# The first front of a two-layer attention and state-space kernel: time steps behind the first rows, square root's table first, a fifth bank, moduli ahead of sines

## The chip, the core and the metric

The kernel runs on one core of a Trainium2 chip. The metric is the time of one execution in device microseconds, as the median of several runs. Traces come from one profiled execution.

## The reference

The input is 2048 rows of 640 numbers. Four blocks follow each other, attention, state space, attention, state space, each on normalised rows and added to its input:

```python
x = x + _A_ref(_layernorm(x), A_wqkv, A_wo)      # 32 heads of 20, softmax(q k' / sqrt(20)) v, times wo
x = x + _B_ref(_layernorm(x), ...)
x = x + _A_ref(_layernorm(x), A_wqkv, A_wo)
x = x + _B_ref(_layernorm(x), ...)

# inside _B_ref: a convolution along the rows with one kernel K per channel d
dt = exp(log_dt)                                  # 640 time steps
A  = -exp(log_A_real) + 1j * A_imag               # 640 x 128
P  = exp((A * dt[:, None])[:, :, None] * pos)     # pos = 0 .. 2047
K  = 2.0 * einsum("dn,dnl->dl", C * dt, P).real
y  = irfft(rfft(u, 4096) * rfft(K, 4096))[:2048] + u * D_skip
```

## The kernel before

Each layer has four stages: a front, the attention proper, the output projection, and the state-space convolution. The kernels K are the same in both layers and depend on the weights alone, so they are made once, by the generator `kgen`, whose steps are woven into the first layer: its small tables are made in the first front, its products during the first attention.

**A front** normalises and transposes the rows. It runs over four groups `i4` of 512 rows (four row tiles `xr` of 128). For a group, VectorE takes the statistics (`ln_stats`: `bn_stats`, `bn_aggr`, then `rstd`: `va`, a square root on ScalarE into `lt`, a reciprocal and one correction into `rs`), and makes `nb`, minus the mean times `rs`. ScalarE applies `rs` and `nb` to each row tile. TensorE transposes the result in five columns `ct` of 128 channels, each into one PSUM tile `pst` of pool S (four buffers). ScalarE copies a column to `xh` (16 bits), and VectorE makes the rest `xl`. Then `block0` makes queries and keys of the first heads (`pq`, also in pool S, 15 products each), and `values4` the values (`pv`) of the group before, in pool M (two buffers, tag `mm`), copied out to `V` by VectorE and ScalarE in parts. Weights go through the same splitting: `stage` loads them and `make` produces `wh` on ScalarE or VectorE and `wl` on VectorE. After the last group the norms of queries and keys give a shift per row (`norms`, `longest`, `shift`), which is written to memory and loaded again as a part of the score operands. The last values end the front.

**The attention** makes a tile `S` of scores on TensorE, its exponential `pt` on ScalarE (128x1024, 2048 of them in both layers) and the weighted values on TensorE. It needs the banks that the front's pools held.

**`kgen`** first loads the tables `lar`, `aim` and `dsk` and the time steps `d5`, and makes the steps' exponential (`exp_exact`: a polynomial on VectorE beside one exponential on ScalarE). The steps go to memory and come back to all partitions (`dt`). Then come, for twelve powers `LV[n]`, `modulus(n)` (one exponential of 128x640 on ScalarE and a transfer to memory, `wd`) and `angle(n)` (four VectorE instructions, a sine and a cosine, both by ScalarE's sine, two transfers). The tiles of each kind have two buffers. `act[0]` ties these ScalarE instructions into one order. When all twelve are done, `load_powers` brings the tables back in another layout (`kpw`), and the attention's filler work starts with them.

**Order.** The program is written in the order of its statements, and a scheduler at compile time orders each engine's instructions: the earlier statement goes first among those that it takes for ready. So `kgen`'s steps fill gaps of the front. `tie(made, before)` adds an order of two instructions without data between them. In the attention all engines' instructions are tied one behind the other. Each engine works through its own queue in order, and SyncE and GpSimd hold the queues of the DMAs. ScalarE holds one set of functions at a time: exponential, sine and square root are in different sets, and a change of set is an instruction of its own, `ACT_TABLE_LOAD`, which the compiler puts ahead of the function that needs it. Copies and scalings run under any set.

Of the kernel before, what the change touches and what calls it, by code (L numbers as in the profile page):

```python
# [11 lines left out]
F32 = mybir.dt.float32  # L12
# [3 lines left out]
AF = mybir.ActivationFunctionType  # L16
ALU = mybir.AluOpType
# [4 lines left out]
P = 128  # L22
# [3 lines left out]
NCT = D // P  # L26
# [11 lines left out]
WS = 256.0  # L38
# [49 lines left out]
def mha_s4d_kernel(ctx, tc, x_in, wqkv, wo, lar, aim, cr, ci, ldt, dsk,  # L88
# [4 lines left out]
    def tie(made, before):  # L93

        if before is not None:
            tc.add_manual_dep(made.ins, before.name, mybir.DependencyInfo(
                mybir.DependencyClass.NoSync, mybir.DependencyReason.DATA), reason="order")
        return made.ins
# [13 lines left out]
    def pst(pool, *a, **k):  # L112
        return ps_[pool].tile(*a, **k)
# [18 lines left out]
    hpi = cp.tile([P, 1], F32, name="hpi")  # L132
# [2 lines left out]
    warm = cp.tile([P, 1], F32, name="warm")  # L135
    ksc = cp.tile([P, 2], F32, name="ksc")
    ve.memset(flag, 0.0)
    with tc.tile_pool(name="op", bufs=1) as op:
        oneh = op.tile([1, L], F16, name="oneh")
        ge.memset(oneh, 1.0)  # L140
        ge.dma_start(onesd, oneh)
# [16 lines left out]
    def rstd(mv, n, pool=sm, tag="rs"):  # L158
# [9 lines left out]
        ve.tensor_mul(rs, rs, t)  # L168
        return rs

    def exp_exact(pool, xx, n):
        k, r, q, z = (pool.tile([P, n], F32, name=f"ee_{t}{n}") for t in "krqz")
        ve.tensor_scalar(z, xx, -100.0, 88.0, ALU.max, ALU.min)
        ve.tensor_scalar(k, z, 1.0 / math.log(2.0), MAGIC, ALU.mult, ALU.add)
        ve.tensor_scalar_sub(k, k, MAGIC)
        ve.scalar_tensor_tensor(r, k, -0.693359375, z, ALU.mult, ALU.add)
        ve.scalar_tensor_tensor(r, k, 2.12194440e-4, r, ALU.mult, ALU.add)
        ve.tensor_scalar_mul(q, r, 1.0 / 5040)
        for cc in (720, 120, 24, 6, 2, 1):
            ve.scalar_tensor_tensor(q, q, 1.0 / cc, r, ALU.add, ALU.mult)  # L180
        se.activation(z, k, AF.Exp, scale=math.log(2.0))
        ve.tensor_scalar_mul(z, z, 1.001)
        zi = z.bitcast(mybir.dt.int32)
        ve.tensor_single_scalar(zi, zi, -8388608, ALU.bitwise_and)
        ve.scalar_tensor_tensor(xx, q, 1.0, z, ALU.add, ALU.mult)
# [12 lines left out]
    def kgen():  # L198
# [22 lines left out]
        yield  # L221
        for n, a in (("cr", cr), ("ci", ci)):
            sy.dma_start(ld[n], a)
        se.activation(ld["lar"], ld["lar"], AF.Exp)
        ve.scalar_tensor_tensor(ld["aim"], ld["aim"], 1.0 / (2 * math.pi), dt, ALU.mult, ALU.mult)
        ve.scalar_tensor_tensor(ld["lar"], ld["lar"], -1.0, dt, ALU.mult, ALU.mult)
        yield
# [114 lines left out]
                ge.dma_start(kd[bs, :].rearrange("(c j) (a b) -> (j a) c b", j=4, b=NB), ko)  # L342

        NE, NSUB, AC = D // BC, BC // DC, 2 * DC
        for n in range(0, NL, 2):
            for f in (modulus, angle):
                for i in range(2):
                    yield from f(n + i)
        for n in ("cr", "ci"):
            ve.scalar_tensor_tensor(ld[n], ld[n], 2.0, dt, ALU.mult, ALU.mult)  # L350
        for k in range(2):
# [69 lines left out]
    def weave(n=0):  # L421

        while filler[0] is not None and not filler[1] and (n > 0 or n == 0 and plan.dve < plan.pe + 0.2):
            step = next(filler[0], "end")
            filler[1] = step == "hold"
            if step == "end":
                filler[0] = None
            if step == "wait":
                break
            n -= n > 0 and (1 if n > 1 else n + 1)  # L430

    def attention(x, stats):
# [50 lines left out]
        def stage(c0, n, tag, dst=None, pool=None):  # L483

            full = QW if pool or tag == "v" else P
            ts = tag + "s" if pool else "ws"
            wt = (pool or q2).tile([P, NCT, QW], F32, tag=ts, bufs=1, name=ts)[:, :, :n]
            cols = c0 if isinstance(c0, tuple) else (c0,)
            m = n // len(cols)
            for k, c_ in enumerate(cols):  # L490
                sy.dma_start(wt[:, :, k * m:k * m + m], wqkv[:, c_:c_ + m].rearrange("(t p) c -> p t c", p=P))

            def make():
                bufs = 1 if tag == "v" else 2
                wh, wl = dst or [q2.tile([P, NCT, full], F16, tag=tag + t, bufs=bufs, name=tag + t)[:, :, :n]
                                 for t in "hl"]
                if not first_layer:
                    ve.reduce_max(wm[:, made[0]:made[0] + 1], wt, axis=AX.XY,
                                  apply_absolute_value=True)
                made[0] += 1  # L500
                if pool:
                    se.activation(wh, wt, AF.Copy, scale=WS)
                else:
                    ve.tensor_scalar_mul(wh, wt, WS)
                ve.scalar_tensor_tensor(wl, wt, WS, wh, ALU.mult, ALU.subtract)
                return wh, wl
            return make
        made = [0]
# [248 lines left out]
        with ExitStack() as c2:  # L757
# [34 lines left out]

            coming = load_x(0)
            made_ = [stage(n * D, P, f"b{n}", wb[n], hp) for n in range(2)]
            if first_layer:
                filler[:2] = kgen(), False
                weave(1)
            sy.dma_start(self_, c_sel)
            for i4 in range(4):
                xr = coming  # L800
                if i4 < 3:
                    coming = load_x(i4 + 1)
                if stats is None:
                    mv, rs = ln_stats(lambda i: xr[i], 4)
                else:
                    mv, rs = stats(i4)
                xn = []
                nb = sm.tile([P, 4], F32, tag="nb", name="nb")
                ve.scalar_tensor_tensor(nb, mv[:, :, 0], -1.0, rs, ALU.mult, ALU.mult)
                for i in range(4):  # L810
                    t = xr[i] if x is None else xp.tile([P, D], F32, tag=f"xr{i}", name=f"xn{i}")
                    se.activation(t, xr[i], AF.Identity, scale=rs[:, i:i + 1], bias=nb[:, i:i + 1])
                    xn.append(t)
                if i4 == 0:
                    for make in made_:
                        make()
                    made_ = [stage(2 * D + q * QW, QW, f"b{q}", [w[:, :, q * QW:q * QW + QW] for w in wv], hp)
                             for q in range(NQ)]
                    ve.tensor_copy(sel, self_)
                for ct in range(NCT):  # L820
                    pt = pst("S", [P, 512], F32, tag="S", name="pst")
                    for i in range(4):
                        te.transpose(pt[:, i * P:i * P + P], xn[i][:, ct * P:ct * P + P], ident)
                    sl = slice(512 * i4, 512 * i4 + 512)
                    se.copy(xh[:, ct, sl], pt)
                    ve.tensor_sub(xl[:, ct, sl], pt, xh[:, ct, sl])
                block0(i4)
                if i4 == 0:
                    for make in made_:
                        make()  # L830
                    nxt.append(stage((P, D + P), 64, "w"))
                else:
                    values4(i4 - 1)
# [960 lines left out]
```

## Time and profile before

| | |
|---|---|
| median of 3 runs | 2644.64 us (2643.77 to 2650.95) |
| span of the profiled execution | 2647.0 us |
| TensorE, ScalarE, VectorE, GpSimd busy | 94%, 89%, 57%, 30% of the span |
| first front, up to the first exponential of the attention | 117.8 us |

The span runs from the first to the last instruction of the profiled execution. No time beside it was recorded for that execution, so its span is its own time here. The rows further down come from the page and from views of the same trace; times are microseconds from the span's start. Line L78 is the helper through which all engines but TensorE are called, so one goes by the names of the tiles.

### The profile page before, as it was taken

The page shows a single profiled execution, that of the slowest core. Times are in us where ns is not written, and L with a number is a line of the kernel's source. Part 1 is how long each engine was busy: PE and PEld are TensorE (multiplying, and loading weights), DVE is VectorE, ACT ScalarE, POOL GpSimd, SP SyncE. Part 2 cuts the span into 40 slices and gives each one's busy share as a digit, 9 for nine tenths or more (in the row PEclk, how much of TensorE's full clock was granted, in tenths as well). Part 3 has the DMA queues.
Part 4 walks back from the last instruction along what each step waited for, and adds up shares of the span by engine and source line. Part 5 has one row for each costly group of instructions (what it writes and reads, how often), then busy time and mean ns, then how long its engine had stood idle before and what let it go on. Part 6 is the DMA issues. An engine that isn't in the chain of part 4 may idle for free.

```text
span 2647.0 us, 118800 instructions
## 1 busy us (share of the span) xinstructions
PE 2492.4 (94%) x52388; PEld 1409.8 (53%) x52388; DVE 1519.5 (57%) x3430; ACT 2344.0 (89%) x2763; POOL 801.7 (30%) x1230
## 2 busy tenths in 40 slices
PE   6899999999999999899898999999999998999898
PEld 3444444454444444587896544454444443444898
DVE  7587777777765887577786323232232222143875
ACT  7899999999999999655665899999999999999574
POOL 1123333233323332111681122222222223222285
PEclk9999999999999999999999999999999999999999
DMA  6522222322222221654652111121121113222466
GB/s 206 189 53 77 68 74 62 82 65 63 61 54 59 53 63 38 234 206 163 213 173 64 47 53 50 51 60 45 45 66 39 50 34 87 71 66 61 137 190 184
DMA packets 188158, 241.99 MB, mean 91 GB/s; under 512 B 43504, under 2 KB 128816, under 8 KB 186224
## 3 DMA queue, kind: packets, MB, share of 16 engines
q1 hardware_dynamic: 151936, 188.28, 22.6%
q0 software_dynamic: 35696, 46.01, 7.4%
q8 instruction: 413, 6.77, 1.1%
q14 instruction: 113, 0.93, 0.1%
HBM read 158.16 MB, written 76.00 MB: 88 GB/s over the span
## 4 chain that ended last, share of the span: by engine, by line
ACT 59%; PE 20%; issue 10%; DVE 3%; DMA 2%; POOL 1%; SPq 0%; ACTq 0%; POOLq 0%; DVEq 0%
ACT pt L78 57%; PE psy L1430 3%; PE pa L903 2%; PE psv L1430 2%; PE po L193 2%; PE psx L1430 2%; PE S L868 2%; PE pst L1452 1%; PE pkx L193 1%; PE pv L586 1%; PE m L620 1%; PE pkt L196 1%; PE pq L773 1%; DMA kb<-khb 1%; DMA kop<-ks 1%
## 5 line engine op out<-in xcount | busy, mean ns | idle before, releaser
L78 ACT ACTIVATE pt<-S 128x1024 f32<-128x1024 f32 x2048 | 1927.7, 1033 | 27.9 <-PE S L868 15.5
L903 PE MATMUL pa<-pt,V 64*32 64x512 f32 x16384 | 1096.9, 589 | 1.4 <-DVE oc L78 1.4
L868 PE MATMUL S<-qop,kop 61*32 61x512 f16 x16384 | 877.2, 380 | 82.7 <-ACT pt L78 67.8
L868 PEld LDWEIGHTS <-kop 61*32 61x32 f16 x16384 | 366.9, 89 | 737.3 <-issue 619.2
L903 PEld LDWEIGHTS pa<-pt,V 64*32 64x32 f32 x16384 | 312.7, 106 | 72.0 <-issue 8.6
L78 POOL DMA_DIRECT2D dn<-oc x248 | 122.7, 501 | 574.2 <-DVE oc L78 574.1
L78 DVE TENSOR_SCALAR qc<-m 128x512 f32<-128x512 f32 (+1 forms) x68 | 46.8, 688 | 312.0 <-PE m L620 312.0
L78 POOL DMA_DIRECT2D db<-dn x248 | 125.4, 512 | 141.5 <-DMA dn<-dr 136.9
L78 POOL DMA_DIRECT2D ot<-oc x256 | 130.5, 517 | 88.4 <-DVE oc L78 55.5
L620 PE MATMUL m<-xl,wh 64*32 64x512 f16 x2560 | 143.8, 376 | 0.3 <-issue 0.3
L620 PE MATMUL m<-xh,wh 64*32 64x512 f16 x2560 | 144.1, 378 | 0.0
L620 PE MATMUL m<-xh,wl 64*32 64x512 f16 x2560 | 143.8, 377 | 0.0
L78 DVE COPY oc<-pa 128x512 f32<-128x512 f32 x64 | 44.2, 690 | 172.9 <-PE pa L903 168.9
L78 ACT COPY xt<-pst 128x1024 f16<-128x1024 f16 x80 | 81.3, 1016 | 60.8 <-PE pst L1452 60.8
L620 PEld LDWEIGHTS <-wh 64*32 64x32 f16 x5120 | 90.3, 93 | 73.3 <-issue 30.8
L78 POOL DMA_DIRECT2D dn<-dr x62 | 34.6, 558 | 287.3 <-DVE dr L78 248.6
L1480 POOL TENSOR_TENSOR kb<-t,kb 128x512 f32<-128x512 f32 x76 | 97.2, 1280 | 65.2 <-DVE t L78 40.8
L78 DVE TENSOR_SCALAR V<-m 128x160 f32<-128x160 f32 x64 | 20.7, 324 | 163.4 <-PE m L586 163.4
L78 DVE TENSOR_TENSOR kb<-ktab 128x512 f32<-128x512 f32 x160 | 106.2, 683 | 0.0
L586 PEld LDWEIGHTS <-xh 128*128 128x128 f16 x960 | 79.7, 98 | 46.7 <-issue 31.4
L1480 POOL TENSOR_TENSOR ka<-ka,kb 128x512 f32<-128x512 f32 x76 | 97.5, 1283 | 6.0
L337 PEld LDWEIGHTS m<-kb,ka 128*32 128x32 f32 x3840 | 60.8, 109 | 71.0 <-issue 52.4
(312 smaller groups left out, 3936.4 us busy)
## 6 DMA issues: line engine op xcount, KB each, us to landing
ka<-kha SPq DMA_DIRECT2D x80, 256.0 KB
kb<-khb SPq DMA_DIRECT2D x80, 256.0 KB
db<-dn POOLq DMA_DIRECT2D x248, 64.0 KB, 3.2
kop<-ks SPq DMA_DIRECT2D x176, 80.0 KB
kpw<-wd POOLq DMA_DIRECT2D x60, 192.0 KB, 3.9
qop<-qs SPq DMA_DIRECT2D x256, 40.0 KB
ot<-oc POOLq DMA_DIRECT2D x256, 40.0 KB, 3.0
kha<-kn SPq DMA_DIRECT2D x20, 512.0 KB
```

Of the source, the lines that this page charges most:

```text
L78: made = f(out, *a, **k)
L193: chain(te.matmul(*a, **k))
L196: chain(te.transpose(*a, **k))
L337: chain(te.matmul(ps[32 * j:32 * j + 32, c8, :], a[n][:, ch, :], b[n][:, dd, :], start=(n == 0), stop=(n == 2), tile_position=(0, 32 * j)))
L586: chain(te.matmul(ps[:, :n], a_[:, ct, sl], m[:, ct, :], start=(k == 0), stop=(k == 14)))
L620: chain(te.matmul(ps[r][32 * t:32 * t + 32, :], a_[rows, ct, 32 * u:32 * u + 32], m[rows, ct, 512 * v:512 * v + 512], start=(k == 0), stop ...
L773: te.matmul(pq, a_[:, ct, :], m[:, ct, sl], start=(n == 0), stop=(n == 14))
L868: chain(te.matmul(S[32 * t:32 * t + 32, 512 * r:512 * r + 512], kt_[rows, kc + 32 * t:kc + 32 * t + 32], qt[rows, :], start=True, stop=Tru ...
L903: chain(te.matmul(pa[r][32 * j:32 * j + 32, :], V[rows, kt, VP * h:VP * h + 32], pts[j // 2][rows, 512 * (j % 2):512 * (j % 2) + 512], sta ...
L1430: at("pe", te.matmul(*a, **k))
L1452: at("pe", te.transpose(pt[:, k, g, :], of_group(x1[k], 4 * q + g), id16))
L1480: at("pool", getattr(ge, f)(*a))
```

## The change

It has six parts:

1. A square root of a constant into `warm` is issued at the program's start, ahead of any other function.
2. In the first layer, `kgen` begins only when the first row group has its `nb` and its normalised rows. The first instruction of `exp_exact` on VectorE is tied behind that `nb`; its exponential and that of `lar` are tied behind the last normalised row of the group. The loads of `lar`, `aim`, `dsk`, `d5` and of the selection table `self` are issued behind the loads of the second row group.
3. In the first layer, the low halves `wl` of the first two weight blocks are tied behind the same `nb`.
4. All twelve moduli come ahead of all twelve angles.
5. Behind the last angle, an exponential of a constant into `warm` is tied.
6. In both layers, the fifth column's transposes go to a tile of pool M (tag `mm`).

```diff
     ve.memset(flag, 0.0)
+    se.activation(warm, hpi, AF.Sqrt)
...
+    begun = [None, None]
+
     def exp_exact(pool, xx, n):
         k, r, q, z = (pool.tile([P, n], F32, name=f"ee_{t}{n}") for t in "krqz")
-        ve.tensor_scalar(z, xx, -100.0, 88.0, ALU.max, ALU.min)
+        tie(ve.tensor_scalar(z, xx, -100.0, 88.0, ALU.max, ALU.min), begun[0])
...
-        se.activation(z, k, AF.Exp, scale=math.log(2.0))
+        tie(se.activation(z, k, AF.Exp, scale=math.log(2.0)), begun[1])
...
-        se.activation(ld["lar"], ld["lar"], AF.Exp)
+        tie(se.activation(ld["lar"], ld["lar"], AF.Exp), begun[1])
...
-        for n in range(0, NL, 2):
-            for f in (modulus, angle):
-                for i in range(2):
-                    yield from f(n + i)
+        for f in (modulus, angle):
+            for n in range(NL):
+                yield from f(n)
+        tie(se.activation(warm, hpi, AF.Exp), act[0])
...
-            def make():
+            def make(after=None):
...
-                ve.scalar_tensor_tensor(wl, wt, WS, wh, ALU.mult, ALU.subtract)
+                tie(ve.scalar_tensor_tensor(wl, wt, WS, wh, ALU.mult, ALU.subtract), after)
...
-            if first_layer:
-                filler[:2] = kgen(), False
-                weave(1)
-            sy.dma_start(self_, c_sel)
+            if not first_layer:
+                sy.dma_start(self_, c_sel)
...
-                ve.scalar_tensor_tensor(nb, mv[:, :, 0], -1.0, rs, ALU.mult, ALU.mult)
+                nb_ = ve.scalar_tensor_tensor(nb, mv[:, :, 0], -1.0, rs, ALU.mult, ALU.mult)
                 for i in range(4):
                     t = xr[i] if x is None else xp.tile([P, D], F32, tag=f"xr{i}", name=f"xn{i}")
-                    se.activation(t, xr[i], AF.Identity, scale=rs[:, i:i + 1], bias=nb[:, i:i + 1])
+                    xn_ = se.activation(t, xr[i], AF.Identity, scale=rs[:, i:i + 1], bias=nb[:, i:i + 1])
                     xn.append(t)
+                if first_layer and i4 == 0:
+                    sy.dma_start(self_, c_sel)
+                    begun[:] = nb_.ins, xn_.ins
+                    filler[:2] = kgen(), False
+                    weave(1)
                 if i4 == 0:
                     for make in made_:
-                        make()
+                        make(nb_.ins if first_layer else None)
...
                 for ct in range(NCT):
-                    pt = pst("S", [P, 512], F32, tag="S", name="pst")
+                    pool, tag = ("M", "mm") if ct == NCT - 1 else ("S", "S")
+                    pt = pst(pool, [P, 512], F32, tag=tag, name="pst")
```

## Rows read from the trace of the kernel before

**Rows 1.** Costliest group: line, engine, operation, tiles, count; busy, mean ns; idle before.

```profile
L78 ACT ACTIVATE pt<-S 128x1024 f32<-128x1024 f32 x2048 | 1927.7, 1033 | 27.9 <-PE S L868 15.5
```

**Rows 2.** Chain of waits, first 120 us: start, duration, what it was.

```profile
100.84 14.01 PE pv L586 x60
...
115.23 0.51 ACT V L78 x2
...
116.50 1.28 ACT L78
...
117.80 1.03 ACT pt L78
```

**Rows 3.** Timeline of the first 20 us: start, duration, engine, what, idle before.

```profile
4.49 0.89 DVE L78 BATCH_NORM_STATS2 st<-xr 128x6 f32<-128x320 f32 x2 [3.59 <-DMA xr<-in_x_in]
...
8.88 0.17 DVE L78 TENSOR_SCALAR ee_z<-k_d 128x5 f32<-128x5 f32 x1 [3.51 <-DMA k_d<-in_ldt]
...
16.33 0.16 DVE L78 SCALAR_TENSOR_TENSOR nb<-mv,rs 128x4 f32<-128x4 f32 x1
...
17.50 2.78 PE L823 MATMUL pst<-ident,xr 128*128 128x128 f32 x11 [17.50 <-ACT xr L78]
```

**Rows 4.** Windows: length; busy PE, PEld, DVE, ACT, POOL; granted clock; DMA share, GB/s.

```profile
0.00:7.00 7.00, 0.00 (x0) 0.00 (x0) 0.98 (x4) 1.28 (x1) 3.35 (x7) 1.00 0.65 205
17.50:115.80 98.30, 90.29 (x449) 46.06 (x449) 75.11 (x180) 82.94 (x132) 5.34 (x8) 0.98 0.60 201
98.10:100.90 2.80, 0.89 (x10) 0.36 (x10) 2.80 (x7) 2.52 (x5) 0.00 (x0) 1.00 0.24 84
100.90:105.40 4.50, 4.50 (x15) 1.80 (x15) 2.13 (x6) 3.97 (x5) 2.05 (x4) 0.62 0.82 311
...
1412.00:1416.00 4.00, 4.00 (x13) 1.45 (x12) 3.71 (x6) 3.64 (x6) 0.00 (x0) 0.57 0.22 71
```

**Rows 5.** Timeline, 15 to 21 us, ScalarE and VectorE.

```profile
15.69 0.74 ACT L78 ACTIVATE k_lar<-k_lar 128x640 f32<-128x640 f32 x1
...
16.58 0.88 DVE L78 BATCH_NORM_STATS2 st<-xr 128x6 f32<-128x320 f32 x2
...
20.53 2.05 ACT L78 CAST xh<-pst 128x512 f16<-128x512 f32 x4 [0.64 <-PE pst L823]
20.71 0.17 DVE L78 TENSOR_SCALAR va<-mv 128x4 f32<-128x4 f32 x1
```

**Rows 6.** Timeline, 94 to 114 us: angles' first VectorE instructions, last sine.

```profile
94.49 0.49 DVE L78 TENSOR_SCALAR kc__1185<-k_aim 128x640 f32<-128x640 f32 x1 [2.34 <-DMA wd<-kc__1159]
...
106.00 0.48 DVE L78 TENSOR_SCALAR kc__1211<-k_aim 128x640 f32<-128x640 f32 x1
...
112.69 0.83 ACT L78 ACTIVATE kc__1221<-kc__1221,hpi 128x640 f32<-128x640 f32 x1
```

**Rows 7.** Groups of instructions, first 118 us.

```profile
L78 ACT ACT_TABLE_LOAD x19 | 24.4, 1283 | 5.5 <-issue 3.8 <-PE S L868 0.8 <-PEq L1783 0.7
```

**Rows 8.** Waits of TensorE, first 118 us: total us, times, longest.

```profile
PE pst L823 <- DVE xl L78: 3.0, 3, 1.4
PE pv L586 <- DVE V L78: 2.1, 3, 0.8
PE nrm L548 <- DVE nsum L78: 1.4, 1, 1.4
```

**Rows 9.** Timeline, 97 to 101 us, ScalarE and VectorE.

```profile
97.82 0.49 DVE L78 TENSOR_SCALAR kc__1185<-ks__1184 128x640 int32<-128x640 int32 x1
...
98.37 1.28 ACT L78 ACT_TABLE_LOAD   x1 [1.96 <-issue]
...
100.31 0.48 ACT L78 ACTIVATE V<-pv 128x160 f32<-128x160 f32 x2
```

**Rows 10.** Timeline of the second front, 1410 to 1412 us.

```profile
1410.79 3.13 DVE L78 TENSOR_TENSOR xl<-pst,xh 128x512 f16<-128x512 f32 x5
...
1411.53 0.66 PE L823 MATMUL pst<-ident,xn 128*128 128x128 f32 x4 [3.51 <-DVE xl L78]
```

## The prediction

> **What bounds the kernel now.** I read the page first: ScalarE's big exponentials are by far the largest group of instructions [rows 1], in two attention stages that keep to ScalarE's pace. The change touches neither. What it can move is when each of them begins, so I turned to the two fronts, first by the chain of waits. The first attention's first exponential starts at 117.80 us, and the chain behind it is simple: sixty value matmuls on TensorE back to back, their copies out of PSUM, one score group, and then a table load of 1.28 us on ScalarE [rows 2]. Before that, TensorE does nothing until 17.50 us [rows 3], and from there to 115.8 it is busy 90.29 of 98.30 us [rows 4]. So the first front is a late start, a nearly full TensorE, 8.0 us of holes and a table load at its end. Whatever comes off it goes off the whole kernel one for one, because the attention behind it runs at ScalarE's pace from its first exponential and its instructions have a fixed order that the front doesn't change.
>
> **Start: the statistics first.** In the timeline VectorE takes the first row tile at 4.49 us and then stands until 8.88, because the time-step instruction next in its queue waits for its load; the statistics resume behind it, mixed with the polynomial of the time steps, and the scale `nb` comes only at 16.33 [rows 3]. The rows were not late: the DMA engines moved 205 GB/s over the first 7 us, 1.43 MB, more than the identity and four row tiles that are asked for first (64 and 4 x 320 KB, 1.38 MB) [rows 4]. Four tiles alone take 4.1 us of VectorE (from 16.58 to `va` at 20.71) [rows 5]. From 4.49 this puts `va` at 8.6. From `va` to the end of `nb` are a small square root and six VectorE instructions of the size of `nb` (0.16 us); with the crossings I estimate 1.7 us, so `nb` ends at 10.3 and not at 16.5 [rows 3]. The square root needs no load any more, since its table comes with the program's first load, which nothing waits for. Gain 6.1 us for TensorE's first transpose.
>
> Not all of that lasts. The exponential of the time steps now stands behind the last normalised row, with its table load: 1.28 us, and two exponentials, 0.2 us for the small one and 0.74 for the table `k_lar`, where today ScalarE idles only 0.64 us before the first `xh` copy [rows 5]. If all of it goes ahead of the copies they are 1.6 us late; if it goes behind them nothing. I take the middle, 0.8: gain 5.3 us, bounds 4.5 and 6.1. The weights' loads are asked for second as before, and the next four row tiles now go ahead of the kernel's two big tables in SyncE's queue, so no row waits longer. GpSimd's load of `d5` moves behind memsets and eight small DMAs; its user now runs after 10 us, which covers that. The low halves of the first weights (two of 0.83 us) are tied behind `nb`, and TensorE wants them only with the third product of a column: nothing.
>
> **End: the exponential's table ahead.** Today the last load stands on the chain, 1.28 us between the score group and the exponential [rows 2]. The new dummy exponential follows the last sine, which ends at 113.5 [rows 6], while ScalarE has holes there. Gain 1.3 us; nothing if the last sine becomes the last thing on ScalarE.
>
> Here a rule speaks on the price. The load at 116.50 us takes 1.28 us, and the exponential follows at 117.80, 0.02 us after its end [rows 2]. The Trainium skill ("ScalarE: Activation LUTs", What ACT_TABLE_LOAD costs) gives about 1.28 us for the load and another 1.38 us of drain with every switch, 2.66 us in all; by that the end would be worth 2.7 us and the sum 11.6. The trace shows no such drain behind the load.
>
> **Middle: moduli first, fifth column elsewhere.** ScalarE makes 19 table loads in the front, 24.4 us [rows 7]. Pairs of moduli and angles alternate, six times two loads; sorted, one exponential stretch and one sine stretch are left, with a square root for three row groups between. I count nine or ten loads after, so some 12 us less of ScalarE. That isn't 12 us of time: ScalarE is off the chain for most of the front. What TensorE loses to others is the bound: 3.0 us in transposes that wait for `xl` to free a bank (the fifth column of each row group, there are four banks), 2.1 for VectorE's copies of values, 1.4 for the norms [rows 8]. The last is the plainest case: ScalarE's copy `V` at 100.31 stands behind a load at 98.37 and a sine [rows 9], TensorE is idle 2 of 2.8 us, and in the next 4.5 us its granted clock is 0.62 on average, mostly the lower of its two levels, 1.2 GHz: 4.5 x 0.38 = 1.7 us lost [rows 4]. Without a load there the hole shrinks, and perhaps with it the dip. The fifth column in the value bank no longer waits for `xl`, but the first product of the next group needs `xh` and `xl` of the first columns anyway, so half of 3.0 is what I count: 1.5. With 0.9 from the norms' hole and 0.6 of the dip, 3.0 us. Bounds: 8.8 us if all holes but the last 0.9 and all of the dip go (8.0 - 0.9 + 1.7); below nothing, a loss of about 3 us, if in three row groups a value tile has to wait 1 us because the fifth column holds one of its two banks (two value copies alone take 0.5 us of ScalarE [rows 2]).
>
> **Second front.** The same edit acts at one place: the fifth transposes wait 3.51 us for `xl`, and the query products stand behind them in TensorE's queue [rows 10]. They can be done earlier, but the second query product needs the first `xl`, and VectorE starts on that only at 1410.79, five of them in 3.13 us [rows 10]. So the queries start perhaps 0.6 us earlier; bounds 0 and 2.3, the latter if the dip to a granted clock of 0.57 over the next 4 us (4 x 0.43 = 1.7 us) goes too [rows 4].
>
> Sum: 5.3 + 1.3 + 3.0 + 0.6 = 10.2 us less. The profiled execution's span is 2647.0 us; which would become 2636.8. The runs' median of 2644.64 lies 2.4 below the span, and so I put the median after at 2634.4 us. A difference under 0.3%, 7.9 us, can't be told from no change here.
>
> **The rivals.** (1) The kernels' chain becomes the end. It starts some 2.5 us later by its time steps, and its steps depend on each other: the temporaries have two buffers, and an angle's first VectorE instruction waits until the transfer two angles before it has landed [rows 6]. If sorting saves only the loads in between and the last sine comes at 110, its load of 1.28 and the exponential stand behind it: 111.6 against 117.8. 6.2 us less, 0.6 in the second front: 2637.8. For it: today the last sine and the last value copy end within 2.5 us of each other. Against it: 12 us less of ScalarE, and moduli need nothing of VectorE. 25%.
>
> (2) The same chain, slower than before. Between the first instructions of two turns lie 11.5 us (94.49 to 106.00), with moduli and loads in them [rows 6]. If the transfers' return sets this and not the loads, six turns of angles take 69 us. Twelve moduli come ahead of them, with 0.74 us for each exponential [rows 5] and a transfer's return of 2.3 us [rows 6] over two buffers some 1.9 us each, 23 in all, from about 38 us: the last sine comes at 130, its load and the first exponential at 132, 14 us later than today: 2659. It decides against the change once the last sine passes 115.8, where its load and the first exponential would end where they do today. Against it: turns shortened by 2.6 us of loads and 1.5 of moduli give 7.4, and the last sine 105. 7%.
>
> (3) The start pays and the rest does not: value tiles and the fifth column take the two banks from each other, a loss of 1 us in each of three groups, and new holes eat what the loads give back: 5.3 + 1.3 - 3 + 0.6, about 4 us: 2640.5. For it: every value tile's two copies are already waited for [rows 8]. 18%.
>
> (4) A switch costs more than its load. Ahead of the load at 98.37 ScalarE idles 1.96 us and the view names no cause [rows 9]. If such a time belonged to every switch, the last one's removal would give 3.2 us and not 1.3: 2632.4. Against it: VectorE's last step for the sine behind that load runs from 97.82 for 0.49 us, up to the load's start, so the load seems to wait with its sine [rows 9]. 3%. The Trainium skill's rule above is of this kind.
>
> **Numbers.** My own case has 47%. Its own range is 2629 to 2637. The range over the cases is 2627 to 2642: the low end takes 5 us more of the holes' bound, the high end takes in (1) and (3) and leaves (2) out. Faster by over 0.3% means under 2636.7: most of my case, all of (4) and a third of (1), 0.56. Slower is (2), 0.07. The rest, 0.37, is within 0.3%.
>
> **What would show it.** TensorE's first transpose at 11 to 12 us; the first square root with no load before it; no load between the first score group and the first exponential; nine or ten loads in the front; the first exponential near 108 us; in the second front no wait of 3.5 us for `xl` at a transpose. The prediction is wrong if ScalarE stands waiting for a sine at the end, if the first `xh` copies are held by the time steps' load for more than 1.6 us, if values wait for the fifth column's bank, or if VectorE waits much longer than today for the kernels' power tables after the attention has begun.

## The result, and the profile after

The changed kernel is slower: 2657.70 us median of 6 runs (2655.47 to 2663.31), ratio to before 1.0047, 95% interval 1.0037 to 1.0057. The ratio is an estimate from the single runs: the six runs of before in the same set had a median of 2648.05 us, and the quotient of the two medians is 1.0036; to the 22 runs of before that came later (2645.36 us) it is 1.0047. The span of the profiled execution is 2658.2 us against 2647.0. The same marks in both traces show where the 11.2 us come from:

| us from the span's start | before | after | difference |
|---|---|---|---|
| TensorE's first transpose | 17.50 | 12.38 | -5.1 |
| TensorE's last value product of the first front | 114.47 | 119.95 | +5.5 |
| last sine of `kgen` (the cosine of the last angle) | 112.69 | 126.91 | +14.2 |
| first exponential of the attention | 117.80 | 123.93 | +6.1 |
| second exponential | 118.72 | 129.14 | +10.4 |
| power tables taken up by VectorE (`kpw`) | 124.93 | 135.72 | +10.8 |
| second front's first transpose | 1404.92 | 1416.68 | +11.8 |
| second attention's first exponential | 1469.26 | 1479.61 | +10.4 |
| end | 2647.0 | 2658.2 | +11.2 |

So after a good start the loss is there by 136 us; the second front gives back 1.4 of it, and the stretches behind the two fronts differ by about as much again. The start, in the timeline of after, ScalarE's rows and then TensorE's:

```profile
9.96 0.21 ACT L78 ACTIVATE lt<-va 128x4 f32<-128x4 f32 x1
...
14.78 1.28 ACT L78 ACT_TABLE_LOAD   x1
16.07 0.21 ACT L78 ACTIVATE ee_z<-ee_k 128x5 f32<-128x5 f32 x1
16.18 2.03 ACT L78 CAST xh<-pst 128x512 f16<-128x512 f32 x4
```

```profile
12.38 4.70 PE L830 MATMUL pst<-ident,xr 128*128 128x128 f32 x20 [12.38 <-ACT xr L78]
17.64 0.38 PE L776 MATMUL pq<-xh,wb 128*128 128x512 f16 x1 [0.57 <-DVE xl L78]
...
23.90 0.38 PE L776 MATMUL pq<-xh,wb 128*128 128x512 f16 x1
33.05 4.71 PE L830 MATMUL pst<-ident,xr 128*128 128x128 f32 x20 [8.77 <-ACT xr L78]
```

The square root needs no load any more and the rows are transposed 5.1 us sooner than in [rows 3]; all twenty transposes go through without a wait for `xl`. But look at the last row: after the first group's queries TensorE stands for 8.77 us until the second group's rows come. In the trace of before it filled this time with eighteen value products, the last of them right ahead of the second group's transposes:

```profile
32.90 0.37 PE L586 MATMUL pv<-wv,xl 128*128 128x480 f16 x1
33.26 0.66 PE L823 MATMUL pst<-ident,xr 128*128 128x128 f32 x4
```

There the transposes began at 33.26, hardly later than here. What holds the second group's rows is VectorE, in its timeline of after:

```profile
26.50 0.16 DVE L78 TENSOR_SCALAR va<-mv 128x4 f32<-128x4 f32 x1
...
29.72 0.82 DVE L78 SCALAR_TENSOR_TENSOR k_aim<-k_aim,k_dt 128x640 f32<-128x640 f32 x1
...
30.64 0.77 DVE L78 SCALAR_TENSOR_TENSOR k_lar<-k_lar,k_dt 128x640 f32<-128x640 f32 x1
...
31.88 0.16 DVE L78 SCALAR_TENSOR_TENSOR nb<-mv,rs 128x4 f32<-128x4 f32 x1
```

From the start of `va` to that of `nb` it takes 5.4 us here and 1.8 in the first group (9.42 to 11.21), because the kernels' big tables and statistics of the third group stand in between in VectorE's queue. So `nb` of the second group starts at 31.88, and in before it started at 32.10: the 5.1 us of the start have not reached the second group. The windows of after give the granted clock there and at one later place (columns as in [rows 4]); from its first transpose at 12.38 up to 115.80, TensorE is busy 87.3 of 103.4 us, before 90.29 of 98.30 [rows 4]:

```profile
24.10:33.05 8.95, 0.18 (x1) 0.00 (x1) 8.70 (x31) 5.59 (x8) 0.00 (x0) 0.69 0.60 177
85.00:89.00 4.00, 4.00 (x11) 1.47 (x11) 3.94 (x7) 0.53 (x1) 0.00 (x0) 0.58 0.43 164
```

The last of these windows is a stretch at a granted clock of 0.58, mostly the lower of the two levels; it begins where a wait of 2.98 us for `xl` ends, at 84.97, the longest of those in the second row of TensorE's waits of after (first 118 us; total, times, longest):

```profile
PE pst L830 <- ACT xr L78: 21.1, 2, 12.4
PE pq L776 <- DVE xl L78: 4.7, 3, 3.0
```

The wait of [rows 8] has only changed its place: 3.0 us at the transposes are now 4.7 at the products behind them.

The larger loss is on ScalarE. There are fewer table loads, as forecast, twelve up to 128 us against nineteen in [rows 7]:

```profile
L78 ACT ACT_TABLE_LOAD x12 | 15.4, 1283 | 0.9 <-PEq L1790 0.7
```

and yet the chain of the kernels ends 14 us later. ScalarE's timeline of after, with the first modulus, two late ones, the first sine and the end of the front:

```profile
31.45 0.74 ACT L78 ACTIVATE ke__1075<-k_lar 128x640 f32<-128x640 f32 x1 [3.07 <-DVE k_lar L78]
...
68.61 0.74 ACT L78 ACTIVATE ke__1099<-k_lar 128x640 f32<-128x640 f32 x1 [1.97 <-DMA wd<-ke__1093]
...
73.39 0.74 ACT L78 ACTIVATE ke__1108<-k_lar 128x640 f32<-128x640 f32 x1 [0.91 <-DMA wd<-ke__1102]
74.15 1.28 ACT L78 ACT_TABLE_LOAD   x1
75.44 0.74 ACT L78 ACTIVATE ks__1111<-ks__1111 128x640 f32<-128x640 f32 x1
...
121.80 0.81 ACT L78 ACTIVATE kc__1212<-kc__1212,hpi 128x640 f32<-128x640 f32 x1
122.63 1.28 ACT L78 ACT_TABLE_LOAD   x1
123.93 1.02 ACT L78 ACTIVATE pt<-S 128x1024 f32<-128x1024 f32 x1
124.97 1.28 ACT L78 ACT_TABLE_LOAD   x1
126.26 0.74 ACT L78 ACTIVATE ks__1221<-ks__1221 128x640 f32<-128x640 f32 x1
126.91 0.81 ACT L78 ACTIVATE kc__1222<-kc__1222,hpi 128x640 f32<-128x640 f32 x1
127.73 1.28 ACT L78 ACT_TABLE_LOAD   x1
129.03 0.20 ACT L78 ACTIVATE warm<-hpi 128x1 f32<-128x1 f32 x1
129.14 2.83 ACT L78 ACTIVATE pt<-S 128x1024 f32<-128x1024 f32 x3
```

Twelve moduli take from 31.45 to 73.39, 3.8 us each; VectorE had the first two angles ready at 35.5 us, and their sines begin at 75.44. From there to the start of the last angle's sine at 126.26 an angle takes 4.6 us. The attention's first exponential runs ahead of the last angle, so two more loads stand between it and the second exponential, and the load that the dummy exponential was to hide lies on ScalarE's path after all. The kernels' power tables are late by about the same amount, 10.8 us.

In the second front the wait of [rows 10] is gone:

```profile
1416.68 3.20 PE L830 MATMUL pst<-ident,xn 128*128 128x128 f32 x20 [1.14 <-DVE st L78]
1423.28 0.38 PE L776 MATMUL pq<-xh,wb 128*128 128x512 f16 x1 [3.40 <-DVE xl L78]
```

The first query product starts 6.60 us behind the first transpose; before it was 7.20:

```profile
1404.92 0.66 PE L823 MATMUL pst<-ident,xn 128*128 128x128 f32 x4 [1.14 <-DVE st L78]
...
1412.12 0.38 PE L773 MATMUL pq<-xh,wb 128*128 128x512 f16 x1
```

### The profile page after: what moved, and what is told of

Read it like the earlier page. It is cut to its first block, busy times and chain, and to the rows that moved or that the text cites. A ratio compares the mean times of both kernels' runs of the same rounds, so it can differ in the third digit from the quotient of the medians.

```text
span 2658.2 us, 118791 instructions
## 1 busy us (share of the span) xinstructions
PE 2495.8 (94%) x52388; PEld 1410.7 (53%) x52388; DVE 1519.7 (57%) x3430; ACT 2335.7 (88%) x2758; POOL 799.8 (30%) x1230
## 4 chain that ended last, share of the span: by engine, by line
ACT 59%; PE 18%; issue 11%; DVE 4%; DMA 2%; POOL 1%; SPq 0%; ACTq 0%; POOLq 0%; DVEq 0%
ACT pt L78 57%; PE psy L1437 3%; PE psv L1437 2%; PE po L196 2%; PE psx L1437 2%; PE pa L910 2%; PE pst L1459 1%; PE S L875 1%; PE pkx L196 1%; PE pkt L199 1%; DMA otl<-ot 1%; PE pq L776 1%; PE pv L589 1%; DMA kop<-ks 1%; DVE x L78 1%
## 5 line engine op out<-in xcount | busy, mean ns | idle before, releaser
L623 PEld LDWEIGHTS <-wh 64*32 64x32 f16 x5120 | 89.7, 94 | 74.2 <-issue 31.2
```

Source lines behind the costliest of these rows:

```text
L623: chain(te.matmul(ps[r][32 * t:32 * t + 32, :], a_[rows, ct, 32 * u:32 * u + 32], m[rows, ct, 512 * v:512 * v + 512], start=(k == 0), stop ...
```

## The experiments

Theory A: sorting makes the kernels' chain longer, because with two buffers of each kind a step waits for the transfer two steps before it, and moduli and angles no longer fill each other's waits; and the fifth column's new bank takes from TensorE the values that filled its wait for the second group. Rivals differ from run to run and stand in the expectations. In the later sets of runs the kernel before took 2645.36 to 2645.65 us (22 to 32 runs); the ratios below are to it. Like the first one they are estimates from the single runs, with a 95% interval, and differ from the quotient of the medians by up to 0.0006.

**Pairs again.** Part 4 undone, the rest of the change kept.

```diff
-        for f in (modulus, angle):
-            for n in range(NL):
-                yield from f(n)
+        for n in range(0, NL, 2):
+            for f in (modulus, angle):
+                for i in range(2):
+                    yield from f(n + i)
```

> The changed kernel with moduli and angles in pairs again (part 4 undone; the exponential behind the last angle stays). Theory: two faults add up, (A) the fifth column in the value pool makes TensorE stand some 8.8 us before the second row group, (B) sorted angles reach past the front, and the last one's two sines with two table loads stand between the attention's first and second exponential. Then here the hole of (A) stays, the last sine comes before the first exponential, the exponentials run without a break from about 120 us, and the time is 5 to 9 us below the changed kernel, about as before. Rival: the chain is late because its time steps wait for the first rows (part 2); then sines still stand behind the first exponential and the time is within 2 us of the changed kernel.

2648.10 us, ratio 1.0009 [1.0000, 1.0019]. The last sine starts at 114.75, its load and the dummy exponential end at 117.1, and the exponentials run from 119.23 without a load between them. TensorE's hole stays (8.40 us). So sorting, with two buffers of each kind, makes some 10 us of the loss; the rest of the change brings nothing either.

**Fifth column back.** Part 6 undone, the rest kept.

```diff
-                    pool, tag = ("M", "mm") if ct == NCT - 1 else ("S", "S")
-                    pt = pst(pool, [P, 512], F32, tag=tag, name="pst")
+                    pt = pst("S", [P, 512], F32, tag="S", name="pst")
```

> The changed kernel with the fifth column back in the first pool (part 6 undone). Theory: TensorE fills the wait for the second row group with value products, the hole of 8.8 us goes, first scores come at some 110 to 114 us; but the angles stay sorted and later than that, so sines and loads stand between the first exponentials, some 4 us each time; in sum 0 to 5 us below the changed kernel. Rival: the hole belongs to the late statistics of the second group and not to the bank; then TensorE still stands 5 us or more there.

2655.84 us, ratio 1.0040 [1.0026, 1.0055]. TensorE's hole is gone (the second group's transposes start at 33.26 without a wait, behind values) and its last value product starts at 107.28, 12.7 us earlier than in after. The time hardly follows, because now three exponentials run between the late angles, 5.1 us apart. ScalarE's timeline of this kernel, one such turn:

```profile
111.58 1.02 ACT L78 ACTIVATE pt<-S 128x1024 f32<-128x1024 f32 x1
112.63 1.28 ACT L78 ACT_TABLE_LOAD   x1
113.92 0.74 ACT L78 ACTIVATE ks__1201<-ks__1201 128x640 f32<-128x640 f32 x1
114.57 0.81 ACT L78 ACTIVATE kc__1202<-kc__1202,hpi 128x640 f32<-128x640 f32 x1
115.40 1.28 ACT L78 ACT_TABLE_LOAD   x1
```

**Fifth column alone.** The kernel before with part 6, the reverse of the diff just shown.

> The kernel before with the fifth column in the value pool alone (part 6 alone). Theory: the twenty transposes of the second row group stand ahead of the first values, TensorE idles 5 to 9 us there, and the kernel is 3 to 9 us slower than before. Rival (the prediction's step): waits for the banks go away and it is 1 to 3 us faster.

2647.53 us, ratio 1.0009 [0.9999, 1.0019]: no difference that can be told, so neither the 3 to 9 us of the theory nor the gain of its rival. The second group's hole is only 4.1 us here, where the first transposes start at 15.60, and TensorE's last value product starts at 111.78, within the 111.17 to 114.47 of the kernels with the old start and the old bank. The new bank costs TensorE where the start is early.

**Sorted alone.** The kernel before with parts 4 and 5.

> The kernel before with moduli ahead of angles and the exponential behind the last angle (parts 4 and 5 alone). Theory: table loads in the front fall to about ten, TensorE's front ends 0 to 3 us earlier, but the last angle's sines stand behind the second exponential with two loads, 4 us of ScalarE; 1 to 5 us slower than before. Rival (the prediction's step): sorting saves ScalarE time and the front ends 2 to 5 us earlier, faster by as much.

2652.39 us, ratio 1.0033 [1.0020, 1.0045]. Sorting is slower by itself, and by more than the 1 to 5 us expected: 11 loads up to 128 us instead of 19, but the last sine starts at 121.04. Two exponentials run ahead of it, from 117.15, and the third starts at 123.28, behind loads at 119.10 and 121.87.

**More buffers.** The change whole, with four buffers shared by moduli and cosines and three for sines, seven in all, instead of two for each kind.

```diff
-            e = p1.tile([P, D], F32, name="ke_")
+            e = p1.tile([P, D], F32, tag="kc_", bufs=4, name="ke_")
...
-            s, c = (p1.tile([P, D], F32, name=f"k{t}_") for t in "sc")
+            s, c = (p1.tile([P, D], F32, tag=f"k{t}_", bufs=3 + (t == "c"), name=f"k{t}_") for t in "sc")
```

> The changed kernel, all six parts, with more buffers for the tables' temporaries: moduli and cosines share four, sines have three, where each kind had two. Theory: the sorted chain is long because each step waits for a buffer to come back from its transfer, and sorting leaves only one kind of buffer in use at a time; with more of them the last sine comes before the attention's first exponential, which starts at 119 to 122 us and runs on without loads between; 6 to 10 us below the changed kernel. Rival: the chain is long because of its place in the queues of VectorE and ScalarE, or of their work; then the last sine still comes behind the first exponential and the time is within 3 us of the changed kernel.

2647.20 us, ratio 1.0006 [0.9997, 1.0015]. ScalarE's timeline:

```profile
72.95 0.74 ACT L78 ACTIVATE ks__1111<-ks__1111 128x640 f32<-128x640 f32 x1 [2.18 <-DVE kc__1112 L78]
...
103.80 0.81 ACT L78 ACTIVATE kc__1222<-kc__1222,hpi 128x640 f32<-128x640 f32 x1
104.63 1.28 ACT L78 ACT_TABLE_LOAD   x1
...
121.76 8.52 ACT L78 ACTIVATE pt<-S 128x1024 f32<-128x1024 f32 x9 [1.64 <-PE S L875]
```

The last sine comes 23.1 us earlier than in after, the exponentials are unbroken, and the 10 us are back. That is theory A's point: the program's order of the steps was the same, only the buffers differ. What sets the end now is TensorE with its hole.

**More buffers, fifth column back.** Both edits.

> As the run before, with the fifth column back in the first pool: the version that should beat both. Theory: no hole of 8.8 us, a chain that ends in time, no load at the first exponential: first exponential at 110 to 113 us, 5 to 8 us less than the kernel before. If the front's end is set by something else yet, it is within 3 us of it.

2644.60 us, ratio 0.9998 [0.9989, 1.0007]. The first exponential comes at 114.93, 6.8 us earlier than with buffers alone; the two differ only in the fifth column's bank. But this is no gain against before, where 5 to 8 us were expected. The angles, freed from their buffers, keep VectorE busy 31.3 of the 34 us from 70 to 104 (24.3 in the pairs with the fifth column back, the next kernel), and TensorE waits for it (waits in the first 118 us):

```profile
PE pst L829 <- DVE xl L78: 5.5, 3, 3.7
PE nrm L551 <- DVE nsum L78: 2.7, 1, 2.7
PE nrm L551 <- DVE V L78: 1.2, 1, 1.2
```

The first of these waits is no larger than in the groups of four and of three below (5.2 and 5.4 us); those of the norms are, 3.9 us in all against 0.8 to 1.3.

**Pairs and fifth column back.** Parts 1, 2, 3 and 5 alone.

> The changed kernel with pairs again and the fifth column back (parts 1, 2, 3 and 5 only), two buffers. Theory: the earlier start lasts, first exponential at 111 to 114 us without a break, 4 to 6 us less than before. Rival: the later time steps put the pairs' last sines at the end of the front; then the first exponential comes at 115 us or later and the time is within 2 us of before.

2645.68 us, ratio 1.0000 [0.9991, 1.0009], where 4 to 6 us less were expected. TensorE's last value product starts at 107.53, 9.7 us earlier than in the pairs with the new bank. The kernels' chain is now the end; ScalarE's timeline:

```profile
112.98 0.81 ACT L78 ACTIVATE kc__1222<-kc__1222,hpi 128x640 f32<-128x640 f32 x1
113.81 1.28 ACT L78 ACT_TABLE_LOAD   x1
115.10 0.20 ACT L78 ACTIVATE warm<-hpi 128x1 f32<-128x1 f32 x1
115.21 2.84 ACT L78 ACTIVATE pt<-S 128x1024 f32<-128x1024 f32 x3
```

TensorE had the first scores done by 110.5 us and waited 5.81 us for the first `pt`. This is rival (1) in its pure form.

**Sines first.** As the last kernel, but all angles ahead of all moduli.

> As the run before, sorted the other way: all angles ahead of all moduli, two buffers. Theory: the chain is as long as the sorted one, but its tail needs the attention's own table, so that late moduli cost 0.7 us each between exponentials and no loads: first exponential at 110 to 113 us, some ten moduli of 0.7 us behind it, and the tables' return is later; from 4 us less to 3 us more than before. Rival: what costs is not the loads but the late return of the tables to VectorE; then it is slower than before by 4 us or more.

2654.08 us, ratio 1.0033 [1.0021, 1.0044]. The first exponential comes early, at 110.09, and no load breaks the row behind it, since moduli use the same table; but moduli run between the exponentials until 124.6, and the power tables come late. VectorE's timeline at its next two steps for them:

```profile
127.28 0.31 DVE L78 MEMSET ktab<- 128x96 f32 x2 [18.83 <-DMA wd<-ke__1228]
132.49 0.56 DVE L78 TENSOR_TENSOR kpw<-kpw 128x384 f32<-128x384 f32 x1 [4.90 <-DMA kpw<-wd]
```

The first attention took 981.2 us from its first exponential to its last, against 969 to 973 in the kernels in which nothing stands between the first exponentials. A late chain costs even without table loads. The time does not tell whether the moduli between the exponentials or the late power tables cost this, but the trace gives the larger part to the moduli: the eighth exponential starts 14.5 us behind the first, in before 8.2, so some 6 of these 10 us are gone ahead of any power table.

**Groups of four.** Buffers, fifth column back, and the loop in groups of four moduli and four angles.

```diff
+        for n in range(0, NL, 4):
+            for f in (modulus, angle):
+                for i in range(4):
+                    yield from f(n + i)
```

> The changed kernel with the fifth column back in pool S, four buffers shared by moduli and cosines, three for sines, and moduli and angles in groups of four: four moduli, then their four angles, three times. It asks whether the chain can end early enough that TensorE sets the end. Theory A (the chain is bound by buffers and transfers, and TensorE's part ends near 109 us once the start is early and its order is the old one): groups of four take 3 times 2 loads where pairs take 12, and moduli overlap with angles, so the last sine comes at 108 or earlier, the first exponential at 110 to 113, nothing breaks the row of exponentials: 2640 to 2643 us, 0.9985 of before or less. Rival B (every saving in the front is met by another of the same size, as with pairs and a fifth column back, 1.0000): the exponential at 115 or, if earlier, followed by later power tables, 2645 to 2647 us.

2646.60 us, ratio 1.0001 [0.9992, 1.0010]. The trace of the front is theory A's (last sine at 108.83, first exponential at 111.45, no load between the exponentials; the first attention ends at 1082.61, before 1088.44), the time is rival B's.

**Groups of three.** The same with three.

> As the groups of four, with groups of three (four times three moduli and three angles): two table loads more, more overlap. Theory A: the last sine between those of the pairs (112.98) and of the groups of four, or like the latter; 2640 to 2644 us. Rival B: 2645 to 2647 us.

2640.01 us, ratio 0.9975 [0.9966, 0.9985], 9 runs: this version is faster than both kernels, by less than the 0.3% that the prediction took as the limit of what can be told, but with an interval clear of 1. ScalarE's timeline:

```profile
108.12 0.82 ACT L78 ACTIVATE kc__1222<-kc__1222,hpi 128x640 f32<-128x640 f32 x1
108.96 1.28 ACT L78 ACT_TABLE_LOAD   x1
110.25 0.20 ACT L78 ACTIVATE warm<-hpi 128x1 f32<-128x1 f32 x1
...
111.62 2.86 ACT L78 ACTIVATE pt<-S 128x1024 f32<-128x1024 f32 x3 [0.79 <-PE S L875]
```

The chain and TensorE's last value product (starting at 108.35) end together, and the power tables are there at 118.51. The front's end is the same as with groups of four within 0.2 us, and the first attention ends at 1083.37, even 0.8 later; yet the medians differ by 6.6 us. In the two traces the difference arises after 1463 us: from the second attention's first exponential to the end it is 1180.0 us with four and 1176.0 with three, 2.1 of it inside the second attention and 1.9 behind it. Over all fourteen traces this stretch lies between 1175.1 and 1180.1 (before 1177.7), with no order that I can see in the front. Why the groups of three come out so much better than the groups of four was not found. Pairs with the seven buffers were not run, so what the grouping gives beside the buffers is open too.

**Sorted with buffers, alone.** The kernel before with parts 4 and 5 and the buffers.

> The kernel before with parts 4 and 5 (moduli ahead of angles, dummy exponential) and with the added buffers (moduli and cosines share four, sines three); start and fifth column as before. Theory A (what sorting costs is the wait of two buffers per kind for their transfers): sorting with buffers costs nothing; last sine before 110, first exponential between 114 and 118 with no table load between exponentials, 2643 to 2646 us, where parts 4 and 5 without buffers took 2652.39. Rival B (sorting itself costs, whatever the buffers, because angles can't begin before the moduli are through): 2650 to 2653 us.

2646.63 us, ratio 1.0001 [0.9992, 1.0010]. The last sine starts at 99.96 and the exponentials run from 115.78 without a load or a break. With enough buffers sorting costs nothing against before, and brings nothing: TensorE's last value product, at 113.84, sets the end.

**End load alone.** The kernel before with part 5.

> The kernel before with part 5 alone, the dummy exponential behind the last sine. Theory A: the 1.28 us load goes from between the first score group and its exponential; the first exponential comes 1.3 us earlier, 2644 us against 2645.4, too little to be told from no change by the median but to be seen in the trace. Rival B (the load goes from the chain but another wait takes its place, or the last sine comes as late as the scores): first exponential at 117.5 or later, 2645.4 us.

2645.89 us, ratio 0.9999 [0.9990, 1.0008]. In the trace the load at 111.35 lies in a hole of ScalarE, and the exponential follows the scores at 114.14 without one, 2.05 us after TensorE's last value product starts; before it is 3.3 (114.47 to 117.80). The 1.3 us are there in the trace and too small for the medians.

## Why the prediction was wrong

**Start: right in sum by luck, and too large for a typical run.** The first transpose came at 12.38, a gain of 5.1 where 6.1 was forecast: VectorE waited 0.65 us for a row tile, and `nb` ended at 11.4 and not at 10.3. Between the last normalised row (ending at 14.76) and the first copy at 16.18 stand the time steps' load and exponential, 1.4 us where it was 0.65 before: a delay of 0.8, as counted. The first query product came at 17.64 instead of 22.80, 5.2 us earlier and near the 5.3 of the sum, but by luck: it starts 5.3 us behind the first transpose in the three kernels with the new start and the new bank, and 5.9 to 6.2 in the six with the new start and the old bank, so the fifth bank gave back what the copies' delay took. And the profiled execution of before was a late one: in four kernels with its start the first transposes begin at 15.49 to 16.59 and not at 17.50, in part because VectorE gets the time steps at 7.7 to 7.9 and not at 8.88 [rows 3]. Against these the gain is 3.1 to 4.2. Its span of 2647.0 us, too, belongs to a time of about 2649 and not to the median of 2644.64, since in all other runs on record the time is 1.7 to 1.9 us longer than the span. With the fifth column in its old bank it does reach the end of TensorE's front: the last value product starts at 107.3 to 108.4 in five kernels with the new start (112.99 in the sixth, where the angles crowd VectorE), and at 111.2 to 114.5 with the old one.

**Middle, moduli first: the step that failed.** I counted 12 us less of ScalarE, let the chain of moduli and angles shrink with it, and gave the longer chain, rival (2), 7%. The longer chain is what happened: the last sine ended 12 us behind the deciding 115.8. That the time is only 1.3 us off the figure of that rival is luck: it had the moduli from 38 us at 1.9 us each and the angles at 5.75 (half a turn of 11.5), and the trace has 31.45, 3.8 and 4.6. The loads went as counted, nine up to 118 us and twelve up to 128, but ScalarE's time in loads was not what the chain lacked. The two estimates behind my "the last sine 105" were both too small: 3.8 us for a modulus instead of 1.9, 4.6 for an angle instead of 3.7 (half a turn of 7.4). I took the old turn of 11.5 us and subtracted the loads and moduli in it. In that turn, however, moduli ran while angles waited for VectorE and for their transfers; sorted, they can't. The chain did not start later, as I had it, but 5.8 us earlier (31.45 against 37.24), and still ended later. The pure test is the pair of runs that differ in buffers alone: 126.91 to 103.80 for the last sine, 10 us in time. Nearly all of it is in the angles: with more buffers the first sine comes 2.5 us earlier (72.95 against 75.44), a modulus still takes 3.2 us, and an angle takes 2.7 instead of 4.6. What makes a modulus dear is mostly something that my 1.9 us left out, the front's own work on ScalarE: from 31.45 to 73.39 in after ScalarE is busy 33.9 of 41.9 us, some 8 of them with moduli. How the buffers act is only partly a wait in the queue: the waits of moduli and angles for transfers in after add up to 7.5 us (2.7 on VectorE, 4.8 on ScalarE). The rest of the 23 us would lie in the order that the scheduler wrote, in which steps that it takes to be waiting for a buffer stand behind other work. That was argued from the traces, not tried by itself.

**Middle, fifth column: the second failure.** I counted 1.5 us of gain and bounded the loss at 3. The loss mechanism that I named, value tiles waiting for a bank, hardly occurs (0.7 us of such waits in after). Instead the transposes of the second group, no longer held by four banks, stand ahead of the values of the first in TensorE's queue, and TensorE waits 8.8 us for rows that are no earlier than before. In the pairs with the new bank TensorE's last value product starts at 117.19, in the pairs with the old one at 107.53. In the changed kernel this stayed hidden behind the late sines: undoing it alone gives 1.9 us.

**End load: right in form.** In the pairs with the new bank and wherever else the chain was in time, no load stands between scores and exponential; in after the condition that I named, the last sine as the last thing on ScalarE, took it away. The Trainium skill ("ScalarE: Activation LUTs", What ACT_TABLE_LOAD costs) adds 1.38 us of drain to each switch; the load at 122.63 takes 1.28 us and its exponential follows 0.02 us after its end, and the load at 124.97 starts 0.02 us after the exponential ahead of it. The trace has no such drain on either side, so rival (4) fell. The Trainium skill ("ScalarE: Activation LUTs", Table sets: the hidden batching unit) asks to batch calls by table set. The runs here do not bear it out: sorting was slower without buffers, 1.0033 with 8 loads fewer, and no faster with them, 1.0001.

**Second front: right.** 0.6 us forecast, 0.6 at the first query product, 1.4 at the attention's first exponential; the wait moved to `pq` (3.40 us for `xl`), as argued. All fourteen traces agree: from the second front's first transpose to its attention's first exponential it is 62.5 to 62.9 us in the four kernels with the new bank and 63.9 to 65.4 in the ten with the old one.

Rivals (1) and (3) are both in the runs too: the chain as the end in the pairs with the fifth column back, and the fifth column eating the start in the pairs with the new bank, though by the order of the transposes and not by value tiles waiting for banks.

**One for one: in the traces up to the second attention, not in the medians.** I had taken it that what comes off the front comes off the whole kernel. In the ten traces with no load, sine or modulus between the first exponentials it is 1349.7 to 1354.1 us from the first exponential to that of the second attention, and behind it the stretch to the end varies by 5 us from kernel to kernel, nearly as much as any version gained in the front. The groups of four had their first exponential 6.3 us earlier than the trace of before and took no less time. What sets that last stretch is open.

## What to carry to other kernels

Before sorting a chain of steps by kind to save table loads, look at how many buffers each kind has and what the steps wait for: here eight loads fewer made the kernel slower with two buffers of each kind, and left its time alone with seven. The one version that was faster, groups of three with seven buffers and the early start, was so for a reason that was not found. A resource that holds work back can be what keeps the queue in a good order; when it is freed, ask what the scheduler will now put first, and what that waits for. And where two chains end within 3 us of each other, shortening one need not show: the start with the end load, the end load alone, and the sorting with buffers each changed the trace and none the time. Shortening both is not enough either, as the groups of four show, so read the stretches behind the front as well.

## What was not expected of the hardware

TensorE's granted clock was 0.69 over the hole of after, from 24.10 to 33.05 us, and 0.58 in the four microseconds behind a wait of 3 us at 85, during which it was busy all the time. That second hole was paid for twice: eleven products fell into these four microseconds, and twenty into the next four, where the clock was 1.00. Behind the first hole the clock was 0.50, the lower level, from 33.05 to 37.75, but the twenty transposes there took 4.71 us, no more than the 4.70 of the first group at 1.00. In the pairs with the fifth column back, where TensorE is busy 89.7 of 95.2 us, the clock is 1.00 over the whole front. Transfers also vary from one execution to the next: VectorE gets the time steps between 7.7 and 8.9 us in five traces whose starts are the same, so a single trace is not good for a microsecond at the start.
